# Attention with random features and a top-1 expert layer: the expert's choice starts ahead of a key maximum, and the second weight matrix of the first expert is rounded later, by ScalarE

## Chip, core and metric

One core of one Trainium2 chip runs the whole program. The metric is the device time of one execution in microseconds (us), the median of several runs. Engines are TensorE (PE), VectorE (DVE), ScalarE (ACT), GpSimd (POOL), and SyncE (SP), which only issues DMAs here.

## What is computed

The reference first computes attention with positive random features, for 8 batches, 8 heads, 576 tokens, head size 64 and 128 features. Its output, read as 4608 tokens of 512 numbers, goes through a layer of 8 experts of which each token uses one.

```python
def phi(x):
    proj = np.einsum('bhsd,md->bhsm', x, omega)
    h = proj - np.sum(x * x, axis=-1, keepdims=True) / 2.0
    h = h - np.max(h, axis=-1, keepdims=True)
    return np.exp(h) / np.sqrt(m)
...
kv = np.einsum('bhsm,bhsd->bhmd', k_p, v)
num = np.einsum('bhsm,bhmd->bhsd', q_p, kv)      # divided by den
...
logits = xn @ en.T / tau
expert_idx = np.argmax(logits, axis=1)
...
h = np.maximum(x[mask] @ w1[e], 0.0)
out[mask] = gate_w[mask, None] * (h @ w2[e])
```

## The kernel before

**Phase 1, attention.** A loop of 43 steps (`i` = 0 to 42) works on 36 tiles of 128 tokens. Step `i` projects key tile `i` and query tile `i - 6` (`proj`), takes the maxima of the features on VectorE (`maxima`, which writes `nmk` or `nmq`), and the exponentials on ScalarE (`feats`, which writes `ftk` or `ftq`). TensorE then transposes the query features (`qtr`, into the PSUM tile `nub`), ScalarE and VectorE copy one half each to SBUF (`qcopy`, which writes `qp`), and TensorE multiplies them with the key-value sums (`num`, into `nub` too). `num_out` divides on VectorE and writes the tokens of tile `i - 7` to a tile `xr` and their logits to `lg`. `kvmm` adds up the key-value sums. Every 4 or 5 steps one of these sums is closed: ScalarE copies it (`kvs`), GpSimd copies it again (`xgp<-kvs`), and TensorE transposes that (`kvtr`) ahead of the next `num`.

**The expert's choice.** Once three tiles have their logits (a group `g`, at steps 9, 12, 15, ...), `routed(g)` runs in pieces that are spread over the next steps. GpSimd adds the logits up (`raw`). VectorE takes their maximum and subtracts it (`mx`, then `raw<-raw,mx`: the first two operations), and GpSimd copies the result into the three `xr` tiles. VectorE picks the expert (three operations with `sel`), TensorE counts with `sel`, and VectorE adds the counts (`base`, `run`). GpSimd turns them into row numbers (four small operations on `base` and `pos`, then `posi`) and scatters each `xr` tile to the buffer `xs` in HBM, with one indirect DMA for each tile, in three successive steps. There are six `xr` buffers, so tile 24, for instance, is written where tile 18 was, once the scatter of tile 18 has landed:

```python
st["xr", i] = xr = p1.tile([P, PAY], F32, name=f"xr{i}", tag="xr", bufs=6)
```

**The first expert's weights.** After group 5 the expert with most tokens so far is known. From step 28 on, its eight pieces of weights of 128x1024 are loaded (`first_weights(n)`; even `n` are the first matrix, odd `n` the second). In the step behind the load, `first_split(n)` rounds each piece to a high part (`w1h` or `w2h`) and lets GpSimd subtract it from the piece in four operations of 128x256 to get the low part (`w1l`, `w2l`). `first_steps` multiplies the first two blocks of tokens with them: its matmuls fill up TensorE from step 37 on and go on behind the loop.

**The order.** Each engine works through its instructions in the order in which the program was written. Pieces that belong to a later step are put in lists: `mid` is played behind `qcopy`, `after` behind `num`, `then` behind the second maximum, ahead of the last key maximum, and `ends` at the end of the step. Pieces of one list run in the order in which they were put there.

**Phase 2, the experts.** From about 218 us on TensorE multiplies tokens with weights, step after step, until shortly before the end.

Of the kernel before, what the change touches and what calls it, by code (L numbers as in the profile page):

```python
# [16 lines left out]
AF = mybir.ActivationFunctionType  # L17
# [12 lines left out]
NTILE = NSB * TPS  # L30
G = 3
REG = N + P
GPICK = 5
# [4 lines left out]
NQ = 4  # L38
# [3 lines left out]
FILLS = 1, 2, 2, 2, 2, 0  # L42
FILL1, FILL2, FILL3 = 6, 11, 6
NSTAT = 38
WARM = 26
NSTEP = 64
XPE = 9
# [8 lines left out]
def attention_moe(ctx: ExitStack, tc: tile.TileContext, qT, kT, v1, omT, emb, tau, w1q, w2q, xs, out):  # L56
    nc = tc.nc
# [221 lines left out]
    with ExitStack() as c1:  # L279
# [243 lines left out]
        def first_weights(n):  # L523

            if n == 0:
                st["fe"] = nc.values_load(firsti[0:1, NPRE + 1 :], engines=[ET.SP], min_val=0, max_val=E - 1, skip_runtime_bounds_check_because=WHY)
            q, wn = n // 2, ("w1", "w2")[n % 2]
            st["rf", n] = raw = rawp.tile([P, F], F32, name=f"rf{n}", tag=f"raw_{wn}")
            nc.sync.dma_start(raw, W[wn][0].rearrange("(e q) p f -> e q p f", q=NQ)[ds(st["fe"], 1), q].rearrange("o p f -> (o p) f"))

        def first_split(n):
            q, (_, h, l) = n // 2, W[("w1", "w2")[n % 2]]
            raw = st["rf", n]
            if n % 2 == 0:
                nc.scalar.activation(h[:, 0, q, :], raw, AF.Copy)
            else:
                nc.vector.tensor_copy(h[:, 0, q, :], raw)
            for c in range(0, F, 256):
                c = slice(c, c + 256)
                nc.gpsimd.tensor_tensor(l[:, 0, q, c], raw[:, c], h[:, 0, q, c].bitcast(F32), op=ALU.subtract)  # L540

        def first_steps():


            new = lambda n, tag: ps.tile([P, 512], F32, name=f"fs_{n}", tag=tag, bufs=2 if tag == "px" else 1)
            hs = {}

            def up(t, a, cs, pa):
                for c in cs:
                    computed("w1", t, products(pa, pre_x[t], "w1", 0, [c], a, c == 0, c == 3))  # L550
                    yield
                if c == 3:
                    nc.scalar.activation(hs[t][:, a * 512 : (a + 1) * 512], pa, AF.Relu)

            def turn(t, a, tag):
                turned(hs[t], a * 512, new(f"h{t}{a}", tag), *(z[:, a * 512 : (a + 1) * 512] for z in pre_h[t]))
                yield

            def down(t, cs, po):
                for c in cs:  # L560
                    computed("w2", t, products(po, pre_h[t], "w2", 0, [c], 0, c == 0, c == 7))
                    yield
                if c == 7:
                    scaled(po, xgp[t], total[:, t : t + 1])
                    store(t, xgp[t])

            n2, total = few("n2", "p", NPRE), few("total", "p", NPRE)
            for t in range(NPRE):
                hs[t] = rawp.tile([P, F], F32, name=f"hp{t}", tag="raw_w1")
                turned(xgp[t], 0, new(f"x{t}", f"kv{t}"), *pre_x[t])  # L570
                squares(xgp[t], n2[:, t : t + 1], hs[t][:, 0:DM])
                yield
            nrm = root(gp, n2, NPRE, "p", nc.gpsimd)
            yield from up(0, 0, range(4), new("a00", "kv0"))
            norms(nrm)
            yield from up(0, 1, range(4), new("a01", "kv1"))
            for t in range(NPRE):
                exps(xgp[t], nrm[:, t : t + 1], total[:, t : t + 1])
            pa = new("a10", "kv0")
            yield from up(1, 0, range(2), pa)  # L580
            yield from turn(0, 0, "kv1")
            yield from up(1, 0, range(2, 4), pa)
            yield from turn(0, 1, "kv1")
            inverted(total)
            yield from up(1, 1, range(4), new("a11", "px"))
            po = new("o0", "kv0")
            yield from down(0, range(4), po)
            yield from turn(1, 0, "kv1")
            yield from turn(1, 1, "px")
            yield from down(0, range(4, 8), po)  # L590
            yield from down(1, range(8), new("o1", "kv1"))
# [47 lines left out]
        mid, after, then, ends = {}, {}, {}, {}  # L639
        at = lambda d, *key: d.setdefault(key, [])  # L640
        for i, f in ((1, emb0), (2, emb1), (4, emb2), (5, emb3)):
            at(ends, i).append((f,))
        later, fill = None, first_steps()

        def go(d, *key):
            for f, *a in d.pop(key, ()):
# [5 lines left out]
        for i in range(END + 1):  # L652
            iq = i - LAG
            st["now"] = i
            n = iq - 3 * GPICK - 7
            if 0 <= n < 2 * NQ:
                first_weights(n)
            if i < 2 or i >= 4:
                load(i + (4 if i < 2 else 2))
            if i in (3, 4):  # L660
                loadq(i - 3)
            loadq(iq + 2 if i > LAG - 1 else -1)
            if iq - 3 * GPICK - 6 == 6:
                prow = [nc.values_load(
                    firsti[0:1, t : t + 1], engines=[ET.SP], min_val=t * P, max_val=(E - 1) * REG + t * P,
                    skip_runtime_bounds_check_because=WHY) for t in range(NPRE + 1)]
                for t in range(NPRE):
                    xload(t, prow[t], xgp[t])
            ks, qs, ts, ss = i < NTILE, 0 <= iq < NTILE, 1 <= iq <= NTILE, 1 <= i <= NTILE
            one, two = [], []  # L670
            if ks and qs:
                one, two = [("k", i, 1, "px"), ("q", iq, 0, "px")], [("k", i, 0, "py"), ("q", iq, 1, "py")]
            elif ks:
                one = [("k", i, a, ("px", "py")[i % 2]) for a in range(2)]
            elif qs:
                two = [("q", iq, a, ("px", "py")[i % 2]) for a in range(2)]
            proj(*one)
            if ts:
                qtr(iq - 1)
            for p in one[:1]:  # L680
                maxima(*p)
            proj(*two)
            if ts:
                qcopy(iq - 1, 1, True)
                qcopy(iq - 1, 0, False)
            go(mid, i)
            for p in one[:1]:
                feats(*p)
            if i == END:
                next(fill)  # L690
            for p in one[1:] or two[:1]:
                maxima(*p)
            if ts:
                num(iq - 1)
            go(after, i)
            for p in two[1:]:
                maxima(*p)
            u = (i - 1) % TPS
            sums = [(j, a, b) for j, b in ([(i - 2, 1)] if u == 5 else []) + [(i - 1, int(u > 4))] for a in range(2)] if ss else []
            if i == LAG:  # L700
                for j, a, b in [x for x in sums if x[1]]:
                    kvmm(j, a, b)
                sums = [x for x in sums if not x[1]]
            go(then, i)
            for p in one[1:] if two else ():
                feats(*p)
            if one:
                for p in two[:1]:
                    maxima(*p)
            for x in sums:  # L710
                kvmm(*x)
            closed = ss and u in (4, 8)
            if closed and not qs:
                kv_closed((i - 1) // TPS, u // 4 - 1)
            if ts:
                num_out(iq - 1)
            for p in (two[::-1] if one else two) or one[1:]:
                feats(*p)
            if closed:
                sb, b = (i - 1) // TPS, u // 4 - 1  # L720
                if qs:
                    kv_closed(sb, b)
                at(mid, i + 1).append((kv_turn, sb, b))
                at(then if i >= LAG else after, i + 1).append((kv_turned, sb, b))
                at(then, i + 1).append((kv_logits, sb, b))
                at(ends, i + 1).append((kv_logits_out, sb, b))
            if ts and iq % G == 0 and iq < NTILE:
                steps = routed(iq // G - 1)
                next(steps)
                for d, key in ((ends, i + 1), (mid, i + 2) if i >= NTILE else (ends, i + 1), (after, i + 2), (ends, i + 2), (ends, i + 2), (ends, i + 3), (ends, i + 4)):  # L730
                    at(d, min(key, END)).append((next, steps, None))
            go(ends, i)
            if NTILE < i <= END:
                for _ in range(FILLS[i - NTILE - 1]):
                    next(fill)
            if 0 <= n < 2 * NQ:
                at(ends, i + 1).append((first_split, n))
        loop.close()
        assert not any((mid, after, then, ends)), (mid, after, then, ends)
        steps = routed(NTILE // G - 1)  # L740
# [179 lines left out]
    with tc.manual_schedule(engines={ET.PE, ET.Activation, ET.DVE, ET.Pool, ET.SP}):  # L920
        xt[NPRE] = pre_x[0]
        turn, ends = {}, NSTAT - 1
# [261 lines left out]
```

## Time and profile before

| | us |
|---|---|
| median of 3 runs (lowest, highest) | 662.74 (662.1, 663.9) |
| profiled execution, its own time | 658.2 |
| its span, first to last instruction | 656.4 |
| PE busy in the span | 631.7 (96%) |
| DVE busy | 497.3 (76%) |
| ACT busy | 416.9 (64%) |
| POOL busy | 328.5 (50%) |

The profiled execution is one run of its own. It was 4.5 us shorter than the median of the timed runs, and 1.8 us of its time lie outside of the span. The granted clock of TensorE was 0.996 of full speed over the span. The busy shares are means over two phases with different limits, so what one place of phase 1 is worth must be read there.

### The profile page before, as it was taken

To read this page: it belongs to the slowest core of one execution; us is meant where nothing else is said; L and a number is where in the kernel's file an instruction comes from. 1 tells how busy PE (TensorE), PEld (TensorE's weight loads), DVE (VectorE), ACT (ScalarE), POOL (GpSimd) and SP (SyncE) were. 2 spreads that over 40 slices of the span, in tenths; PEclk is the share of its full clock that TensorE was granted. 3 is DMA by queue.
4 is the path that set the end of the run, shared out by engine and by line. 5 is a ranking of instruction groups with operands and counts; after the bars stand their busy time and mean duration, and the time that the engine had idled before them with its cause. 6 is when DMAs were issued, how large, how long until landed. Compare 5 with 4: busy or idle time off the path is not lost. (4 is left out here: it accounts for less than half of the span.)

```text
span 656.4 us, 18641 instructions
## 1 busy us (share of the span) xinstructions
PE 631.7 (96%) x6339; PEld 532.1 (81%) x6340; DVE 497.3 (76%) x952; ACT 416.9 (64%) x1074; POOL 328.5 (50%) x414
## 2 busy tenths in 40 slices
PE   8999999998889999999999999999999999999993
PEld 7899999988877787888788888888888888888872
DVE  4789888899888736778787777777768787777771
ACT  6899899899877236645656565656555656565430
POOL 2013443448885425474556364646455554646352
PEclk9999999999999999999999999999999999999998
DMA  7547667678832388588898888978697878887710
GB/s 252 177 148 228 196 202 212 214 243 285 261 125 97 118 308 259 156 237 198 237 211 223 208 227 190 240 193 232 178 244 184 236 192 196 225 208 212 187 64 34
DMA packets 142362, 131.89 MB, mean 201 GB/s; under 512 B 106742, under 2 KB 106870, under 8 KB 142272
## 3 DMA queue, kind: packets, MB, share of 16 engines
q1 hardware_dynamic: 135808, 110.04, 62.8%
q0 software_dynamic: 6320, 20.38, 7.9%
q8 instruction: 57, 0.93, 0.6%
q10 hardware_dynamic: 144, 0.26, 0.2%
q14 instruction: 33, 0.27, 0.1%
HBM read 83.78 MB, written 21.97 MB: 161 GB/s over the span
## 5 line engine op out<-in xcount | busy, mean ns | idle before, releaser
L241 PE MATMUL nu<-w2h,hl 128*128 (+1 forms) x288 | 113.9, 395 | 0.4 <-DVE hl L948 0.4
L241 PE MATMUL nu<-w2h,hh 128*128 (+1 forms) x288 | 113.9, 396 | 0.0
L241 PE MATMUL nu<-w2l,hh 128*128 (+1 forms) x288 | 113.8, 395 | 0.0
L241 PE MATMUL pa<-w1h,xl 128*128 (+1 forms) x280 | 110.8, 396 | 0.4 <-DVE xl L947 0.4
L241 PE MATMUL pa<-w1h,xh 128*128 (+1 forms) x280 | 111.1, 397 | 0.0
L241 PE MATMUL pa<-w1l,xh 128*128 (+1 forms) x280 | 110.6, 395 | 0.0
L909 ACT ACTIVATE pl<-pa 128x512 uint16<-128x512 uint16 x68 | 40.1, 594 | 94.2 <-PE pa L241 56.0
L905 DVE TENSOR_REDUCE wd<-t 128x1024 uint16<-128x1024 uint16 x68 | 90.0, 1325 | 1.7 <-DMA t<-pl 1.7
L338 ACT ACTIVATE ftk<-pjk,nmk 128x128 f32<-128x128 f32 x288 | 84.9, 427 | 6.3 <-DVE nmk L331 6.0
L207 POOL TENSOR_TENSOR w1l<-raww,w1h 128x1024 f32 x34 | 83.7, 2461 | 7.4 <-DVE w1h L206 5.5
L905 DVE TENSOR_REDUCE pl<-pa 128x512 uint16<-128x512 uint16 x68 | 46.6, 688 | 51.6 <-ACT pl L909 51.5
L338 ACT ACTIVATE ftq<-pjq,nmq 128x128 f32<-128x128 f32 x288 | 80.0, 430 | 8.7 <-DVE nmq L331 7.8
L207 POOL TENSOR_TENSOR w2l<-raww,w2h 128x1024 f32 x34 | 82.1, 2415 | 2.4 <-issue 2.4
L327 PE MATMUL pjq<-om,qt 64*128 64x128 f32 x576 | 75.6, 283 | 1.1 <-ACT ftk L338 0.7
L327 PE MATMUL pjk<-om,kt 64*128 64x128 f32 x576 | 76.3, 285 | 0.3 <-DVE om L602 0.3
L944 ACT ACTIVATE hh<-wd 128x1024 fp32r<-128x1024 f32 x34 | 36.1, 1062 | 60.2 <-DVE wd L905 54.3
L327 PEld LDWEIGHTS pjk<-om,kt 64*128 64x128 f32 x576 | 65.1, 190 | 2.9 <-DVE om L602 0.6
L271 POOL DMA_INDIRECT y<-xgp x20 | 22.7, 1136 | 87.6 <-DVE xgp L248 84.1
L241 PEld LDWEIGHTS nu<-w2h,hl 128*128 128x128 f32 x288 | 54.0, 188 | 13.9 <-DVE hl L948 0.8
L327 PEld LDWEIGHTS pjq<-om,qt 64*128 64x128 f32 x576 | 63.9, 188 | 1.6 <-ACT ftk L338 0.9
L241 PEld LDWEIGHTS nu<-w2l,hh 128*128 128x128 f32 x288 | 54.1, 188 | 13.1
L241 PEld LDWEIGHTS nu<-w2h,hh 128*128 128x128 f32 x288 | 54.1, 188 | 13.0
(311 smaller groups left out, 1270.0 us busy)
## 6 DMA issues: line engine op xcount, KB each, us to landing
raww<-w1q SPq DMA_DIRECT2D x38, 512.0 KB, 3.9
raww<-w2q SPq DMA_DIRECT2D x38, 512.0 KB, 5.2
qt<-qT SPq DMA_DIRECT2D x36, 256.0 KB, 4.3
kt<-kT SPq DMA_DIRECT2D x35, 256.0 KB, 3.0
xgp<-xs SPq DMA_DIRECT2D x20, 260.5 KB, 2.8
xg<-xs SPq DMA_DIRECT2D x18, 260.5 KB, 2.9
rf<-w1q SPq DMA_DIRECT2D x4, 512.0 KB, 5.6
rf<-w2q SPq DMA_DIRECT2D x4, 512.0 KB
```

The costliest lines, as they stand in the source:

```text
L207: il = nc.gpsimd.tensor_tensor(at(l, dp), raw, at(h, dp).bitcast(F32), op=ALU.subtract)
L241: done.append(nc.tensor.matmul(dst, x[:, c * P : (c + 1) * P], ws.rearrange("p o f -> p (o f)"), start=(begin and i == 0 and k == 0), stop ...
L271: w = nc.gpsimd.indirect_dma_start(out=out, out_offset=bass.IndirectOffsetOnAxis(ap=xg[:, PAY - 1 : PAY].bitcast(I32), axis=0), in_=xg[:, ...
L327: nc.tensor.matmul(st["pj" + w, i, a][:, c, :], st[w, i][r, c, :], om[r, :], start=True, stop=True)
L338: nc.scalar.activation(ft[:, h, :], pj[:, h, :], AF.Exp, bias=nm[:, h : h + 1])
L905: nc.vector.tensor_reduce(to, src.unsqueeze(2), axis=AX.X, op=ALU.max)
L909: nc.scalar.activation(planes[1][:, o : o + 512], halved(src)[:, :, 1], AF.Copy)
L944: nc.scalar.activation(hh, wd[:, 0:F], AF.Relu)
```

## The change

The expert's choice: for groups whose choice starts before step 36, the first two operations on VectorE and the three copies on GpSimd move from the end of the step to the list `then`, ahead of the last key maximum. The weights: two tables now say in which step each piece is loaded (behind that step's keys, values and queries instead of ahead of them) and in which step and list it is split. The pieces of the first matrix keep their steps, the pieces of the second matrix are split in steps 37, 38, 40 and 41. ScalarE rounds all of them. As the splits are now entered into the lists before the loop starts, they run ahead of the other pieces of the same list.

```diff
+WLOAD = {28: (0,), 30: (2, 1), 32: (4, 3), 34: (6,), 39: (5,), 40: (7,)}
+WSPLIT = {0: (1, 29), 2: (1, 31), 4: (1, 33), 6: (1, 35), 1: (0, 37), 3: (0, 38), 5: (0, 40), 7: (0, 41)}
...
         def first_split(n):
             q, (_, h, l) = n // 2, W[("w1", "w2")[n % 2]]
             raw = st["rf", n]
-            if n % 2 == 0:
-                nc.scalar.activation(h[:, 0, q, :], raw, AF.Copy)
-            else:
-                nc.vector.tensor_copy(h[:, 0, q, :], raw)
+            nc.scalar.activation(h[:, 0, q, :], raw, AF.Copy)
...
-        later, fill = None, first_steps()
+        for n, (late, i) in WSPLIT.items():
+            at(ends if late else mid, i).append((first_split, n))
+        fill = first_steps()
...
-            n = iq - 3 * GPICK - 7
-            if 0 <= n < 2 * NQ:
-                first_weights(n)
             if i < 2 or i >= 4:
                 load(i + (4 if i < 2 else 2))
             if i in (3, 4):
                 loadq(i - 3)
             loadq(iq + 2 if i > LAG - 1 else -1)
+            for n in WLOAD.get(i, ()):
+                first_weights(n)
...
-                for d, key in ((ends, i + 1), (mid, i + 2) if i >= NTILE else (ends, i + 1), (after, i + 2), (ends, i + 2), (ends, i + 2), (ends, i + 3), (ends, i + 4)):
+                for d, key in ((then if i < NTILE else ends, i + 1), (mid, i + 2) if i >= NTILE else (ends, i + 1), (after, i + 2), (ends, i + 2), (ends, i + 2), (ends, i + 3), (ends, i + 4)):
                     at(d, min(key, END)).append((next, steps, None))
...
-            if 0 <= n < 2 * NQ:
-                at(ends, i + 1).append((first_split, n))
```

Three places show how instructions move. The first is GpSimd in steps 29 to 31. A number behind a name is that of the tile or group: `rf0` is piece 0 of the weights, `xr18` the tokens of tile 18, `base6` belongs to group 6. Before:

```order
L484 TENSOR_TENSOR base6_3628<-base6_3628,sel0_127 128x24
L449 TENSOR_TENSOR base6_3628<-base6_3628 128x3x4
L449 TENSOR_TENSOR base6_3628<-base6_3628 128x3x2
L449 TENSOR_TENSOR pos6_3632<-base6_3628 128x3
L494 CAST posi06_3636<-pos6_3632 128x1
L496 DMA xs<-xr18_3047,posi06_3636 38016x576
L540 TENSOR_TENSOR w1l_107<-rf0_3356,w1h_106 128x256 x4
L425 COPY xr23_3744<-ids_89 128x1
L449 TENSOR_TENSOR lg7_3472<-lg7_3472 128x3x32
```

The same place of the changed kernel:

```order
L539 TENSOR_TENSOR w1l_107<-rf0_3362,w1h_106 128x256 x4
L486 TENSOR_TENSOR base6_3631<-base6_3631,sel0_127 128x24
L451 TENSOR_TENSOR base6_3631<-base6_3631 128x3x4
L451 TENSOR_TENSOR base6_3631<-base6_3631 128x3x2
L451 TENSOR_TENSOR pos6_3635<-base6_3631 128x3
L496 CAST posi06_3639<-pos6_3635 128x1
L498 DMA xs<-xr18_3053,posi06_3639 38016x576
L427 COPY xr23_3744<-ids_89 128x1
L451 TENSOR_TENSOR lg7_3478<-lg7_3478 128x3x32
```

The four subtractions of piece 0 moved from behind the scatter of tile 18 to a place ahead of the whole chain that leads to it.

The second place is VectorE in step 31, from the key maximum to the query copy of step 32. Before:

```order
L331 TENSOR_REDUCE nmk_0_3855<-pjk_0_3811 128x4
L429 TENSOR_SCALAR rr_3876<-nub 128x8
L430 RECIPROCAL rr_3876<-rr_3876 128x8
L432 TENSOR_TENSOR xr_3873<-nub,rr_3876 128x2x4x64
L435 TENSOR_TENSOR lg_3875<-nub,rr_3876 128x64
L459 TENSOR_REDUCE mx_3896<-raw_3761 128x3
L460 TENSOR_TENSOR raw_3761<-raw_3761,mx_3896 128x24
L465 SCALAR_TENSOR_TENSOR sel_128<-raw_3761,iotm 128x24
L466 TENSOR_REDUCE mx_3896<-sel_128 128x3
L467 TENSOR_TENSOR sel_128<-iotm,mx_3896 128x24
L331 TENSOR_REDUCE nmk_1_3944<-pjk_1_3918 128x4
L405 COPY qp_0_3958<-nub 128x512
```

The same place of the changed kernel (`xr_3872` is tile 24 here, as `xr_3873` is before):

```order
L461 TENSOR_REDUCE mx_3843<-raw_3761 128x3
L462 TENSOR_TENSOR raw_3761<-raw_3761,mx_3843 128x24
L333 TENSOR_REDUCE nmk_0_3854<-pjk_0_3804 128x4
L431 TENSOR_SCALAR rr_3875<-nub 128x8
L432 RECIPROCAL rr_3875<-rr_3875 128x8
L434 TENSOR_TENSOR xr_3872<-nub,rr_3875 128x2x4x64
L437 TENSOR_TENSOR lg_3874<-nub,rr_3875 128x64
L467 SCALAR_TENSOR_TENSOR sel_128<-raw_3761,iotm 128x24
L468 TENSOR_REDUCE mx_3843<-sel_128 128x3
L469 TENSOR_TENSOR sel_128<-iotm,mx_3843 128x24
L333 TENSOR_REDUCE nmk_1_3939<-pjk_1_3913 128x4
L407 COPY qp_0_3953<-nub 128x512
```

The two operations on `mx` and `raw` went ahead of the key maximum; the casts `w2h<-rf`, which stood at the end of steps 30, 32, 34 and 36, are gone from this engine.

The third place is GpSimd in steps 35 and 36, up to the copy of the last key-value sum. Before:

```order
L484 TENSOR_TENSOR base8_4478<-base8_4478,sel0_127 128x24
L449 TENSOR_TENSOR base8_4478<-base8_4478 128x3x4
L449 TENSOR_TENSOR base8_4478<-base8_4478 128x3x2
L449 TENSOR_TENSOR pos8_4482<-base8_4478 128x3
L494 CAST posi08_4486<-pos8_4482 128x1
L496 DMA xs<-xr24_3873,posi08_4486 38016x576
L540 TENSOR_TENSOR w1l_107<-rf6_4228,w1h_106 128x256 x4
L425 COPY xr29_4564<-ids_89 128x1
L363 COPY xgp2_105<-kvs3_1_4581 128x2x4x64
```

The same place of the changed kernel:

```order
L539 TENSOR_TENSOR w1l_107<-rf6_4218,w1h_106 128x256 x4
L486 TENSOR_TENSOR base8_4464<-base8_4464,sel0_127 128x24
L451 TENSOR_TENSOR base8_4464<-base8_4464 128x3x4
L451 TENSOR_TENSOR base8_4464<-base8_4464 128x3x2
L451 TENSOR_TENSOR pos8_4468<-base8_4464 128x3
L496 CAST posi08_4472<-pos8_4468 128x1
L498 DMA xs<-xr24_3872,posi08_4472 38016x576
L427 COPY xr29_4545<-ids_89 128x1
L365 COPY xgp2_105<-kvs3_1_4562 128x2x4x64
```

Here too the subtractions, of piece 6, went ahead of the chain and its scatter; the copy of the key-value sum stays behind all of them.

## Rows read from the trace of the kernel before

**Rows 1.** Phase 2: its length, then PE, PEld, DVE, ACT, POOL busy, clock, DMA.

```profile
218.00:640.00 422.00, 420.59 (x1838) 337.65 (x1837) 314.38 (x490) 230.86 (x427) 220.98 (x120) 1.00 0.79 208
```

**Rows 2.** Waits of PE, 140 to 225 us: in total, times, longest.

```profile
PE nub L417 <- DVE qp L405: 4.0, 5, 1.7
```

**Rows 3.** Groups of instructions, 140 to 225 us: busy, mean ns, idle before.

```profile
L537 DVE CAST w2h<-rf 128x1024 fp32r<-128x1024 f32 x4 | 3.5, 862 | 0.0
```

**Rows 4.** Waits of ACT, 151 to 173 us (steps 30 to 33).

```profile
ACT qp L405 <- PE nub L400: 1.5, 2, 0.9
```

**Rows 5.** Timeline of POOL, steps 29 to 31: start, duration, idle before.

```profile
146.97 0.19 POOL L425 COPY xr<-ids 128x1 int32<-128x1 int32 x1 [3.38 <-DMA xs<-xr,posi]
148.04 0.23 POOL L484 TENSOR_TENSOR base<-base,sel 128x24 f32<-128x24 f32 x1 [0.89 <-DVE base L481]
...
150.23 1.05 POOL L496 DMA_INDIRECT xs<-xr,posi  x1 [0.86 <-POOL posi L494]
...
155.53 0.24 POOL L449 TENSOR_TENSOR raw<-lg 128x24 f32<-128x24 f32 x1
...
157.31 2.79 POOL L540 TENSOR_TENSOR w2l<-rf,w2h 128x256 fp32r<-128x256 f32 x4
```

**Rows 6.** Timeline of ACT, steps 29, 35: `w1h` is the rounding.

```profile
148.62 1.14 ACT L535 ACTIVATE w1h<-rf 128x1024 fp32r<-128x1024 f32 x1
...
179.78 1.14 ACT L338 ACTIVATE ftk<-pjk,nmk 128x128 f32<-128x128 f32 x4 [1.30 <-DVE nmk L331]
...
184.06 1.14 ACT L535 ACTIVATE w1h<-rf 128x1024 fp32r<-128x1024 f32 x1
```

**Rows 7.** Scatters `xs<-xr,posi` issued from 140 to 166 us, issue to landing.

```profile
DMA to landing us min/median/max: 5.5/5.8/6.5
```

**Rows 8.** The same of the scatters issued from 204 to 222 us.

```profile
DMA to landing us min/median/max: 2.7/2.8/2.8
```

**Rows 9.** Timeline of DVE, step 31.

```profile
157.82 0.69 DVE L432 TENSOR_TENSOR xr<-nub,rr 128x512 f32<-128x512 f32 x1
...
158.56 0.17 DVE L459 TENSOR_REDUCE mx<-raw 128x3 f32<-128x24 f32 x1
...
159.50 0.65 DVE L465 SCALAR_TENSOR_TENSOR sel<-raw,iotm 128x24 bf16<-128x24 f32 x1
...
160.39 0.18 DVE L467 TENSOR_TENSOR sel<-iotm,mx 128x24 bf16<-128x24 f32 x1
...
161.09 0.68 DVE L405 COPY qp<-nub 128x512 f32<-128x512 f32 x1
```

**Rows 10.** Timeline of DVE, end of step 34.

```profile
176.61 0.17 DVE L459 TENSOR_REDUCE mx<-raw 128x3 f32<-128x24 f32 x1
...
177.47 0.65 DVE L465 SCALAR_TENSOR_TENSOR sel<-raw,iotm 128x24 bf16<-128x24 f32 x1
...
178.46 0.69 DVE L537 CAST w2h<-rf 128x1024 fp32r<-128x1024 f32 x1
```

**Rows 11.** Timeline of POOL, steps 36 and 37.

```profile
185.37 1.05 POOL L496 DMA_INDIRECT xs<-xr,posi  x1 [0.56 <-POOL posi L494]
...
189.84 0.60 POOL L363 COPY xgp<-kvs 128x512 f32<-128x512 f32 x1
```

**Rows 12.** Timeline of PE, step 37.

```profile
190.49 0.66 PE L372 MATMUL kvtr<-ident,xgp 128*128 128x128 f32 x4 [0.32 <-POOL xgp L363]
```

**Rows 13.** Waits of ACT, 189 to 213 us (steps 37 to 41).

```profile
ACT ftq L338 <- DVE nmq L331: 6.1, 5, 1.8
```

**Rows 14.** Waits of POOL, 190 to 226 us.

```profile
POOL base L484 <- DVE base L481: 4.1, 2, 3.2
POOL xs L496 <- DVE runi L761: 3.2, 1, 3.2
```

**Rows 15.** Timeline of POOL behind the loop.

```profile
231.57 0.60 POOL L765 DMA_DIRECT2D xs<-w1l  x1 [5.08 <-DMA xgp<-xs]
```

**Rows 16.** Timeline of PE at the start of phase 2.

```profile
232.02 0.60 PE L227 MATMUL fs_x<-ident,xgp 128*128 128x128 f32 x4
```

## Prediction

> **What bounds the kernel now.** I read the chain that ended last first; it covers only the last microseconds, so the bound must be read by stage. The table of busy time by stretch shows phase 2: TensorE is busy for 420.59 of 422 us [rows 1]. Whatever phase 1 gains or loses is therefore carried to the end nearly whole, and the change touches phase 1 alone.
>
> In phase 1 I read the waits of each engine and then the timelines. Two views have to be held against each other. TensorE waits for VectorE's query copy (`qp`), 4.0 us in five waits [rows 2], and VectorE spends 3.5 us on the four casts that the change takes away [rows 3]. That looks like a gain. But from 151 to 173 us ScalarE has only two waits, 1.5 us together, both for TensorE [rows 4]: it goes through its exponentials and roundings without a pause, so most of what VectorE saves there meets ScalarE. The third engine to watch is GpSimd. It is far from busy on the whole, but in steps 28 to 37 it holds things that others need: the copy for `kvtr`, the sums `raw`, and the scatters that free the `xr` buffers. A copy into an `xr` tile has already stood still for 3.38 us, waiting for a scatter to land [rows 5].
>
> **The change, part by part.** The sum is made against the profiled execution (658.2 us) and put on the median of the runs shown, 662.74 us, which lies 4.5 us above it.
>
> *Casts taken from VectorE.* In steps 30, 32 and 36 I count them at nothing, since ScalarE or TensorE ends the waits there [rows 4]. If that cover were gone, each would be worth its 0.86 us [rows 3]. In step 34 the cast is on the path: ScalarE then waits 1.30 us for the key maximum behind it [rows 6]. Before that maximum stand `mx` and `raw<-raw,mx` (176.61 to 177.47), a `sel` of 0.65 us and the cast of 0.69 us [rows 10]. The first pair moves ahead at a cost of about 0.4 us, `sel` no longer meets a split on GpSimd (undisturbed, an operation of that size took 0.18 us [rows 9]) and the cast is gone: some 1.5 us less, of which ScalarE can use the 1.30 us that it waits. **-1.3 us.**
>
> *First two operations ahead of the key maximum, steps 10 to 28.* VectorE does the same work; the maximum and what follows come about 0.4 us later, and `sel` follows at the old time. Up to step 28 I find no wait that this lengthens by more than 0.1 us a group. Seven groups: between 0 and +0.7 us, taken as 0, since the query copy of the next step does not move.
>
> *Split of piece 0 ahead of the scatter of tile 18 (step 29).* This is the largest term. GpSimd was at the chain `base` at 148.04 us and issued the scatter at 150.23 [rows 5]. Now the split comes first, and it must wait for ScalarE's rounding, which ends at 148.62 + 1.14 = 149.76 [rows 6]. Four subtractions take 2.79 us when nothing disturbs them [rows 5]: 152.6. The chain up to the issue took 150.23 - 148.04 = 2.19 us: 154.8. Around here a scatter lands 5.5 to 6.5 us after its issue, 5.8 in the middle [rows 7]: 160.6. VectorE writes tile 24 into the same buffer two steps later, at 157.82 before [rows 9]. It will stand there until 160.6, and GpSimd too, whose copy into tile 24 waits for the same landing. Behind the write, the distance to the query copy of step 32 was 161.09 - 157.82 = 3.27 us; `mx` and `raw` (158.56 to 159.50, 0.94 us) are gone from it, but `sel` stays slow, because the split of piece 2, held up by the same landing, then runs beside it [rows 9]. So the copy comes at 160.6 + 2.33 = 162.9 instead of 161.09. **+1.8 us.** Upper end: a landing after 6.5 us (+0.7) and a second `sel` operation slowed from 0.18 to 0.65 us (+0.5). Lower end: the shortest landing that any row shows, 2.8 us [rows 8], at 157.6: no wait at all, 0. I take the middle of the landings in this stretch, since the second matrix is loaded in the same stretch as before and now right behind the first, so it is no emptier.
>
> The Trainium skill, page "DMA: Bandwidth & Descriptors", section "Anatomy of one DMA — SWDGE (gpsimd) path", gives such a DMA a fixed 2.0 us plus its bytes over 436e3 per us; for 128 rows of 521 numbers that is an estimate of 2.6 us. The quiet stretch agrees (2.8), the stretch in question does not (5.8). By the page the scatter would land at 157.4 and the sum would be that of the second rival below.
>
> *Split of piece 6 ahead of the chain (step 35).* Rounded at 184.06 + 1.14 = 185.20 [rows 6], split until 188.0, the chain 1.9 us more (2.19 less 0.30 for the shorter pause of 0.56 ahead of the issue), the issue 1.05, one small copy 0.2: the copy for `kvtr` starts at 191.1 instead of 189.84 [rows 11]. TensorE already waits 0.32 us for it [rows 12], and the next `num` stands behind `kvtr`. **+1.3 us.** The split that went away from step 34 does not help, as GpSimd caught up before.
>
> *Four roundings more on ScalarE, steps 37 to 41.* At 1.14 us each [rows 6] they stand between `qp` and `ftq`, where ScalarE waits 6.1 us in five waits for the query maximum [rows 13]. About 1.2 us a step cover about 1.1: **0**, and up to 0.5 us where the cover is short.
>
> *Four splits in steps 37 to 41 on GpSimd.* One takes the place of the split that stood in step 37, three are added: 3 x 2.79 = 8.4 us. GpSimd's idle time there is 4.1 + 3.2 = 7.3 us [rows 14]. So the last scatters come about 1.1 us later, and with them the load of the third block of tokens, which waits for them all. That block landed at about 231.5 (GpSimd's DMA at 231.57 waited for it [rows 15]), and TensorE takes it up at 232.02 [rows 16]: 0.5 us of slack. **+0.5 us.** Operations on VectorE that meet these splits: between 0 and twice 0.47 us; **+0.3 us.**
>
> Sum: -1.3 + 1.8 + 1.3 + 0.5 + 0.3 = **+2.6 us**, 665.3 us.
>
> **Rivals.** *The scatter lands in time.* At anything under about 4 us the buffer is free when VectorE comes. Then `mx` still waits for `raw`, whose end (155.77 before [rows 5]) moves by the 4.6 us of the scatter less the 2.79 us or more of the split that stood between, to about 157.3; this takes away what the shorter `sel` gives, and the query copy is about where it was. The sum is -1.3 + 1.3 + 0.5 + 0.3 = +0.8 us, 663.5 us. For it speaks [rows 8], against it [rows 7].
>
> *VectorE is the bound of steps 30 to 36 after all (faster).* Then its four casts come back whole: -3.5 us [rows 3], 659.2 us. For it speak TensorE's waits [rows 2], against it ScalarE without pauses [rows 4]. It is decided at step 35: the gain must still stand when `kvtr` starts, so the copy on GpSimd must not come after 189.84 less the gain.
>
> *ScalarE waits for the late loads.* The last two pieces are loaded in steps 39 and 40, one step ahead of their rounding. If they take as long as loads did in the crowded stretch (5.8 us as the scatters [rows 7]) instead of a step, ScalarE stands for about 1.5 us ahead of `ftq`; with the second case that is +2.3 us, 665.0 us. Against it: DMA is quiet there [rows 8].
>
> **How the numbers follow.** About 0.3%, 2.0 us, is what a measurement of this kernel can tell from no change. Chances: forecast 0.55, scatter in time 0.27, VectorE the bound 0.11, late loads 0.07. The forecast's own range is 664.0 to 667.0: the landing and the slow `sel` at their upper ends (+1.2) and the tail whole (+0.5) above, a landing at 5.5 us and no disturbance by splits (-0.6), with part of the chain's pause hidden, below. About a fifth of it lies under +2.0. Slower: 0.8 x 0.55 + 0.6 x 0.07 = 0.48. Faster: the third case, and it alone: 0.10. The rest, 0.42, is no change to be told. The range for 8 in 10 takes in the second case with its own spread down to 661.6 and ends above at 667.0; it leaves out the third case and a few mishaps above.
>
> **What would show it.** In the profile after: VectorE's write to `xr` in step 31 with an idle stretch of about 2 us ended by a scatter's DMA; GpSimd's first split right behind ScalarE's first rounding; no wait of 1.3 us for the key maximum in step 35; `kvtr` waiting for GpSimd for 1 us or more in step 37; ScalarE's waits for the query maximum in steps 37 to 41 nearly gone. The prediction is wrong if the scatter of tile 18 lands within about 4 us, or if its write in step 31 has no such wait.

## The result and the profile after

The change makes the kernel slower: 666.84 us (median; 665.38 to 669.33) against 662.84 us (662.1 to 663.9) of the kernel before on the same chip, a ratio of 1.0059, 95% interval 1.0037 to 1.0081. The prediction named 665.3 us, with a range of 661.6 to 667.0, and slower as the likeliest outcome. But the 4.0 us are not the sum that it worked out. They are a loss of some 9 us in the weights part and a gain of some 5 us in the part that it had counted at nothing.

A number that comes up throughout: the runs fell on several chips, and the kernel before takes 663 us on some of them (662.8, 663.6 and 663.1 in the three comparisons) and 657 us on others (657.05 and 656.8). Below they are called a 663 chip and a 657 chip, and medians are compared on one chip alone. Each chip on record served one comparison, so whether the chip itself makes the difference, or something else of that comparison, is not shown; the names only sort the runs. The profiled execution shown ahead of the prediction (658.2 us) looks like one of a 657 chip; the experiments show why this matters.

The profile after was taken on an execution of 669.33 us (span 667.5), 2.5 us above its median. Line numbers are 2 higher than before. First VectorE in step 31, its timeline (start, duration, idle before and what ended it), the answer to [rows 9]:

```profile
159.11 0.18 DVE L461 TENSOR_REDUCE mx<-raw 128x3 f32<-128x24 f32 x1 [0.28 <-POOL raw L451]
159.32 0.18 DVE L462 TENSOR_TENSOR raw<-raw,mx 128x24 f32<-128x24 f32 x1
159.43 0.68 DVE L333 TENSOR_REDUCE nmk<-pjk 128x4 f32<-128x512 f32 x1
...
166.01 0.69 DVE L434 TENSOR_TENSOR xr<-nub,rr 128x512 f32<-128x512 f32 x1 [5.59 <-DMA xs<-xr,posi]
...
167.17 0.39 DVE L469 TENSOR_TENSOR sel<-iotm,mx 128x24 bf16<-128x24 f32 x1
...
168.08 0.67 DVE L407 COPY qp<-nub 128x512 f32<-128x512 f32 x1
```

The two moved operations stand ahead of the last key maximum (159.11). The write to `xr`, which did not wait before, now waits 5.59 us for a scatter. GpSimd's timeline of steps 29 to 31 shows which, beside [rows 5]:

```profile
152.18 2.79 POOL L539 TENSOR_TENSOR w1l<-rf,w1h 128x256 fp32r<-128x256 f32 x4 [3.40 <-ACT w1h L536]
...
156.82 1.05 POOL L498 DMA_INDIRECT xs<-xr,posi  x1 [0.57 <-POOL posi L496]
...
165.97 0.19 POOL L427 COPY xr<-ids 128x1 int32<-128x1 int32 x1 [4.92 <-DMA xs<-xr,posi]
```

The split of piece 0 comes first, the scatter of tile 18 behind it at 156.82. The copy into tile 24, which needs that scatter to have landed, goes on at 165.97, 9.15 us after the issue. TensorE stands still meanwhile; its waits from 143 to 228 us (total, times, longest) answer to [rows 2] and [rows 12]:

```profile
PE nub L402 <- DVE lg L437: 6.4, 2, 5.8
...
PE kvtr L374 <- POOL xgp L365: 1.1, 1, 1.1
PE nub L419 <- DVE qp L407: 0.8, 2, 0.6
```

The wait for the query copy fell from 4.0 to 0.8 us, and others took its place: 5.8 us of step 31 in one piece, and 1.1 us for `kvtr` in step 37 (0.32 before). In steps 37 to 41 ScalarE, the answer to [rows 13]:

```profile
ACT ftq L340 <- DVE nmq L333: 1.8, 3, 1.2
...
ACT w2h L536 <- DMA rf<-w2q: 0.5, 1, 0.5
```

Phase 2 lasts as long as before: from the query copy of step 42 (225.93) to the end of the span (667.5) it is 441.6 us, against 442.1. All that differs lies in phase 1.

### The profile page after: what moved, and what is told of

It is laid out like the page before. It is cut to its first block, busy times and chain, and to the rows that moved or that the text cites. A ratio compares the mean times of both kernels' runs of the same rounds, so it can differ in the third digit from the quotient of the medians.

```text
span 667.5 us, 18640 instructions
## 1 busy us (share of the span) xinstructions
PE 634.8 (95%) x6339; PEld 534.0 (80%) x6340; DVE 492.3 (74%) x948; ACT 420.2 (63%) x1078; POOL 325.3 (49%) x414
```

## The experiments

All code lines are against the kernel that the heading names. Experiments 1 to 4 ran on one 663 chip (before: 663.62 us, 662.63 to 666.33).

**1. Changed kernel, the four splits of the first matrix behind the routed pieces again.**

```diff
+BEHIND = 0, 2, 4, 6
-            at(ends if late else mid, i).append((first_split, n))
+            if n not in BEHIND:
+                at(ends if late else mid, i).append((first_split, n))
...
+            for n in BEHIND:
+                if WSPLIT[n][1] == i:
+                    at(ends, i).append((first_split, n))
             go(ends, i)
```

> The changed kernel, with the four splits of the first matrix put behind the routed pieces of their steps again, as they stood before. Theory: the 4.0 us come from the order on GpSimd (the split of piece 0 ahead of the scatter of tile 18, that of piece 6 ahead of the copy for kvtr); then both waits go, step 31 takes about 6 us and not 11.5, and the median falls by 4 to 6 us, to 661 to 663. Rival, the first two operations ahead of the key maximum cost about 2 us by step 28: 664 to 665. Rival, the roundings and splits in steps 37 to 41 cost the time: 665 or more.

Measured: 660.12 us, ratio to before 0.9948 (0.993 to 0.9966), a little under the time expected. The order alone is worth more than the whole loss; the changed kernel with the old order beats the kernel before. The profile has neither wait: step 31 takes 5.50 us, and `kvtr` does not wait. It was taken on the slowest of the eight executions, though (662.79 us), and has another loss: steps 32 and 33 take 17.70 us, against 12.05 in experiment 2. TensorE stands still for 2.06 us in step 32, for a load of queries, and its clock falls (last section).

**2. Kernel before, with the two operations moved and nothing else.**

```diff
-                for d, key in ((ends, i + 1), (mid, i + 2) if i >= NTILE else (ends, i + 1), (after, i + 2), (ends, i + 2), (ends, i + 2), (ends, i + 3), (ends, i + 4)):
+                for d, key in ((then if i < NTILE else ends, i + 1), (mid, i + 2) if i >= NTILE else (ends, i + 1), (after, i + 2), (ends, i + 2), (ends, i + 2), (ends, i + 3), (ends, i + 4)):
```

> The kernel before with one part of the change alone: the first two operations of the expert's choice ahead of the last key maximum. Theory: nothing to tell, 662.5 to 663.5; the 2.1 us by which the changed kernel was behind at step 28 in its profiled execution are its spread. Rival, the move costs about 2 us in steps 10 to 28: 664.5 to 665.5.

Measured: 658.77 us, ratio 0.9923 (0.9903 to 0.9943). Both expectations fail, and in sign: the move gains 4.9 us.

**3. Changed kernel without that move.**

```diff
-                for d, key in ((then if i < NTILE else ends, i + 1), (mid, i + 2) if i >= NTILE else (ends, i + 1), (after, i + 2), (ends, i + 2), (ends, i + 2), (ends, i + 3), (ends, i + 4)):
+                for d, key in ((ends, i + 1), (mid, i + 2) if i >= NTILE else (ends, i + 1), (after, i + 2), (ends, i + 2), (ends, i + 2), (ends, i + 3), (ends, i + 4)):
```

> The changed kernel without the move of the first two operations: the weights part alone. Theory: it carries the whole loss, 666 to 668. Rival, the move costs 2 us: 664.5 to 665.5.

Measured: 672.72 us, ratio 1.0135 (1.0115 to 1.0154). The weights part alone loses 9.1 us, more than either expectation allowed. The two parts account for the change: 0.9923 x 1.0135 = 1.0057, against 1.0059 measured.

**4. Changed kernel, the split of piece 0 alone behind the routed pieces:** experiment 1 with a shorter list.

```diff
-BEHIND = 0, 2, 4, 6
+BEHIND = 0,
```

> The changed kernel, with the split of piece 0 alone put behind the routed pieces of step 29. Theory: the wait of 5.6 us in step 31 goes; what the profiled step 31 lost (11.5 against 6.2 us) and step 32 (1.2 us) comes back in part, 662 to 664; the wait for the copy for kvtr in step 37 (1.1 us) stays. Rival, the stall of step 31 would have been made up elsewhere (GpSimd's load sets the end of phase 1): 665.5 or more.

Measured: 661.07 us, ratio 0.9958 (0.9942 to 0.9975). By the two ratios, both of 663 chips, this one place gives back 1.0059 - 0.9958 = 0.0101, 6.7 us. Its profile has no wait in step 31 and the old wait in step 37; VectorE's timeline, then TensorE's waits from 185 to 220 us:

```profile
157.88 0.69 DVE L435 TENSOR_TENSOR xr<-nub,rr 128x512 f32<-128x512 f32 x1
...
159.74 0.68 DVE L408 COPY qp<-nub 128x512 f32<-128x512 f32 x1
```

```profile
PE kvtr L375 <- POOL xgp L366: 1.6, 1, 1.6
```

Between 4 and 1 stand the splits of pieces 2, 4 and 6: 0.0010, 0.7 us, less than the two intervals can tell apart.

Why does a move of two small operations gain 4.9 us where the profile before showed no wait that it could shorten? The program of experiment 3 is, up to step 27, that of the kernel before, and it was profiled on the 663 chip. VectorE's waits there, from 27 to 137 us:

```profile
DVE rr L431 <- PE kva L355: 2.3, 2, 1.2
DVE rr L431 <- ACT ftq L340: 2.0, 3, 1.1
...
DVE rr L431 <- PE nub L419: 1.0, 2, 0.5
DVE rr L431 <- PE nub L386: 1.0, 1, 1.0
```

Together 6.3 us ahead of `rr`, the first operation on a finished `num`. Step 13 of the same profile shows what stands behind that wait, and below it step 13 of experiment 2:

```profile
60.67 0.17 DVE L431 TENSOR_SCALAR rr<-nub 128x8 f32<-128x8 f32 x1 [0.52 <-PE nub L419]
...
61.90 0.17 DVE L461 TENSOR_REDUCE mx<-raw 128x3 f32<-128x24 f32 x1
62.11 0.18 DVE L462 TENSOR_TENSOR raw<-raw,mx 128x24 f32<-128x24 f32 x1
...
63.50 0.67 DVE L407 COPY qp<-nub 128x512 f32<-128x512 f32 x1
```

```profile
59.04 0.17 DVE L459 TENSOR_REDUCE mx<-raw 128x3 f32<-128x24 f32 x1
59.24 0.18 DVE L460 TENSOR_TENSOR raw<-raw,mx 128x24 f32<-128x24 f32 x1
...
59.94 0.15 DVE L429 TENSOR_SCALAR rr<-nub 128x8 f32<-128x8 f32 x1
...
62.47 0.68 DVE L405 COPY qp<-nub 128x512 f32<-128x512 f32 x1
```

In the old place the pair stands between the wait and the query copy of the next step, with no pause behind it. In the new place it fills the time in which VectorE would wait. The same waits in experiment 2:

```profile
DVE rr L429 <- PE kva L353: 2.3, 2, 1.1
...
DVE rr L429 <- PE nub L384: 0.7, 1, 0.7
```

3.0 us instead of 6.3; the repetition, experiment 12, has 3.0 us as well.

**5 and 6. Kernel before, unchanged, profiled again.** These, 7 and 8 ran on a 657 chip (before: 657.05 us, 655.43 to 658.24).

> The kernel before, unchanged, profiled once more: its first profiled execution (658.2) lay under all of its timed runs. Theory: in an execution of its usual time, 663, the steps in which the expert's choice stands ahead of the query copy (13, 16, 19, 22, 25, 28) are longer than in the first profile by 0.5 to 1 us each, as the weights part alone shows them (13: 5.82 against 5.17; 16: 5.81 against 5.15; 22: 6.42 against 5.23; 25: 5.86 against 5.15). Rival: the 5 us lie in phase 2 or ahead of step 7, and the steps are as in the first profile.

> The kernel before, unchanged, a third profiled execution, for the spread between executions. The same expectations as for the second.

Measured: 658.01 and 658.18 us, so not executions of 663 us as hoped; but they show the same thing from the other side. VectorE's waits ahead of `rr`, 27 to 138 us, in experiment 5:

```profile
DVE rr L429 <- ACT ftq L338: 0.9, 3, 0.3
DVE rr L429 <- PE nub L384: 0.2, 1, 0.2
```

1.1 us against 6.3 for the same program. From the query copy of step 7 to that of step 28 it takes 138.27 - 27.32 = 110.95 us here, 111.20 in experiment 6 and 111.08 in the profile ahead of the prediction, but 142.48 - 27.25 = 115.23 in experiment 3. These are the rows:

```profile
27.32 0.68 DVE L405 COPY qp<-nub 128x512 f32<-128x512 f32 x1
138.27 0.68 DVE L405 COPY qp<-nub 128x512 f32<-128x512 f32 x1
```

```profile
27.25 0.68 DVE L407 COPY qp<-nub 128x512 f32<-128x512 f32 x1
142.48 0.68 DVE L407 COPY qp<-nub 128x512 f32<-128x512 f32 x1
```

The steps named in the expectation (13, 16, 19, 22, 25) are longer by 0.6 to 1.2 us each between experiments 5 and 3. With the move the stretch takes 138.33 - 27.08 = 111.25 us on the 663 chip: 4.0 of the 4.9 us lie in these steps. No profile of the kernel before itself was taken on a 663 chip; experiment 3 stands in for it up to step 27.

**7. Changed kernel, the load of piece 1 one step later.**

```diff
-WLOAD = {28: (0,), 30: (2, 1), 32: (4, 3), 34: (6,), 39: (5,), 40: (7,)}
+WLOAD = {28: (0,), 30: (2,), 31: (1,), 32: (4, 3), 34: (6,), 39: (5,), 40: (7,)}
```

> The changed kernel with the load of piece 1 one step later (31 and not 30), so that it no longer stands right behind that of piece 2. Theory: the scatter of tile 18 landed 9.1 us after its issue since both loads ran beside it; apart from that load it lands after 5.5 to 6.5 us, the wait in step 31 falls from 5.6 to about 3 us, and the median to 663.5 to 665. Rival: the landing is late for another reason (the scatters, key and value loads alone): 666 to 667.5, with a wait of 5 us or more in step 31.

Measured: 661.57 us, ratio 1.0057 (1.0038 to 1.0077). The expected times were for a 663 chip and can't be held against a 657 chip; the wait in step 31 can: 3.00 us, as the theory has it. Experiments 9 and 10 put both kernels on one chip.

**8. Kernel before, the two operations moved in steps 10 to 25 alone:** experiment 2 with another bound.

```diff
-                for d, key in ((then if i < NTILE else ends, i + 1), (mid, i + 2) if i >= NTILE else (ends, i + 1), (after, i + 2), (ends, i + 2), (ends, i + 2), (ends, i + 3), (ends, i + 4)):
+                for d, key in ((then if i < 27 else ends, i + 1), (mid, i + 2) if i >= NTILE else (ends, i + 1), (after, i + 2), (ends, i + 2), (ends, i + 2), (ends, i + 3), (ends, i + 4)):
```

> The kernel before with the two operations ahead of the last key maximum in steps 10 to 25 alone; in steps 28, 31 and 34 they stay where they were. Theory: the gain of the move (4.9 us) is made in the steps before the weights, some 0.7 us in each of six: 659 to 660.5. Rival: it is made in steps 28 to 34, where VectorE casts and meets GpSimd's splits: 662.5 or more.

Measured: 655.93 us, ratio 0.9984 (0.9974 to 0.9995). On a 657 chip the move gains 1.1 us in these steps: there is little wait to fill. The times named were those of a 663 chip, so this run does not test the rival; the 4.0 us by place, under 5 and 6, speak against it.

**9 and 10. The changed kernel beside the one with the later load**, on another 657 chip (before: 656.8 us, 655.19 to 658.24). The edit is that of experiment 7.

> The changed kernel, unchanged, beside the kernel with the later load. The kernel before took 663.6 us on one chip and 657.05 on another; on a chip of the second kind the sum of the parts (split order about +6, late splits +1.4, the move about -1.5) gives a ratio of 1.008 to 1.010, on one of the first kind 1.006 as measured. Rival: the chip changes the level alone, and the ratio is 1.006 on both.

> The changed kernel with the load of piece 1 one step later, on the same chip as the changed kernel. Theory: the two loads side by side lengthen the landing of the scatter of tile 18; with the later load the wait in step 31 is 3 us and not 5.6, and the time 2 to 3.5 us under that of the changed kernel. Rival: the load makes no difference to be told (within 1 us); the landing is late because of the scatters, the key and value loads.

Measured: 664.11 us, ratio 1.0089 (1.0057 to 1.0121), and 660.5 us, ratio 1.005 (1.0033 to 1.0067). The ratio of 9 is where the sum of the parts had it, but its interval takes in the rival's 1.006. One of its six executions took 658.23 us, at a granted clock of 0.995 where the other five have 0.989 to 0.992, so the loss is not in every execution; that one has no profile. The later load takes 3.6 us off the median. The two intervals overlap a little, so this rests on the traces as well. First experiment 9: SyncE issues both loads as GpSimd issues the scatter of tile 18, and VectorE waits 6.21 us (timelines of SP's queue, POOL, DVE).

```profile
152.54 0.34 SPq L531 DMA_DIRECT2D rf<-w1q  x1
153.14 0.34 SPq L531 DMA_DIRECT2D rf<-w2q  x1
```

```profile
153.14 1.05 POOL L498 DMA_INDIRECT xs<-xr,posi  x1 [0.56 <-POOL posi L496]
...
162.93 0.19 POOL L427 COPY xr<-ids 128x1 int32<-128x1 int32 x1 [5.55 <-DMA xs<-xr,posi]
```

```profile
162.98 0.69 DVE L434 TENSOR_TENSOR xr<-nub,rr 128x512 f32<-128x512 f32 x1 [6.21 <-DMA xs<-xr,posi]
```

Then experiment 10, the same rows:

```profile
151.88 0.34 SPq L531 DMA_DIRECT2D rf<-w1q  x1
...
156.95 1.26 SPq L531 DMA_DIRECT2D rf<-w2q  x1
```

```profile
152.64 1.05 POOL L498 DMA_INDIRECT xs<-xr,posi  x1 [0.56 <-POOL posi L496]
...
159.41 0.19 POOL L427 COPY xr<-ids 128x1 int32<-128x1 int32 x1 [2.54 <-DMA xs<-xr,posi]
```

```profile
159.45 0.69 DVE L434 TENSOR_TENSOR xr<-nub,rr 128x512 f32<-128x512 f32 x1 [3.20 <-DMA xs<-xr,posi]
```

From issue to landing it is 162.93 - 153.14 = 9.8 us with both loads beside it, and 159.41 - 152.64 = 6.8 us with the second load 4.3 us behind the scatter. The scatter itself is the same. The other profiles agree: 9.15 us in the profile after and 9.55 in experiment 3, with both loads; 6.6 us in experiment 7.

**11 and 12. The changed kernel with order and loads mended, beside the move alone**, on a 663 chip (before: 663.11 us, 661.1 to 665.02). 12 is experiment 2 again; 11 is experiment 1 with two loads moved.

```diff
-WLOAD = {28: (0,), 30: (2, 1), 32: (4, 3), 34: (6,), 39: (5,), 40: (7,)}
+WLOAD = {28: (0,), 30: (2,), 31: (1,), 32: (4,), 33: (3,), 34: (6,), 39: (5,), 40: (7,)}
```

> The changed kernel with both mends: the four splits of the first matrix behind the routed pieces of their steps, and the loads of pieces 1 and 3 one step later. Theory: what is left against the move alone is the late roundings and splits in steps 40 and 41, 1 to 2 us: ratio to the kernel before 0.994 to 0.996 on a chip where that takes 663, 0.998 to 1.001 on one where it takes 657. Rival: with order and loads mended the casts off VectorE pay too, and it is under the move alone by 1 us or more.

> The move of the two operations alone, once more beside the mended kernel. Theory: it beats the kernel before on every chip, by 4.9 us again where that takes 663, by 1 to 2 us where it takes 657. Rival: on a chip of 657 it makes no difference (within 0.5 us).

Measured: 659.74 us, ratio 0.9952 (0.9936 to 0.9968), and 657.37 us, ratio 0.9912 (0.9893 to 0.9932). With the order mended the later loads bring nothing more that the medians show (0.9948 in experiment 1). What is left of the weights part still costs 2.4 us against the move alone, so as a whole it does not pay. Where it costs them is shown in part only, since the profile of 11 is of its shortest execution (657.11 us): steps 28 to 36 take 49.28 us there against 50.63 in 12, and steps 37 to 41 take 27.20 against 26.11. Casts and late splits were not run apart. The fastest version on 663 chips is the kernel before with the move alone. The whole move ran on 663 chips only; on a 657 chip the part of it in experiment 8 is 1.1 us faster.

## Why the prediction came near, and what was wrong in it

The profiles put the time in its places. Lengths in us between query copies, and to the end of the span:

| steps | before, 657 chip (exp. 5) | changed, 657 chip (exp. 9) | move alone, 663 chip (exp. 2) | changed, 663 chip |
|---|---|---|---|---|
| 7 to 27 | 110.95 | 109.52 | 111.25 | 112.52 |
| 28 to 30 | 16.93 | 15.93 | 16.70 | 16.41 |
| 31 to 33 | 18.12 | 25.24 | 18.14 | 24.58 |
| 34 to 36 | 16.08 | 16.11 | 15.77 | 16.03 |
| 37 to 41 | 25.01 | 28.06 | 26.16 | 28.78 |
| 42 to end | 441.8 | 441.5 | 440.8 | 441.6 |

On the 657 chips the lengths add up to +7.5 between the first two columns, where the medians differ by 7.3 us. In the last column TensorE waits 1.10 us in step 22, as in no other profile here.

**First two operations ahead of the key maximum, "taken as 0": this step failed.** The range given for it reached from nothing to +0.7 us and had no gain in it. Measured for the whole move: -4.9 us, and -5.7 us in the repetition, on 663 chips; of this -4.0 us in steps 7 to 27, where a 657 chip has -1.4 us. The step reasoned from a profile of 658.2 us, in which VectorE hardly waits ahead of `rr`, about a kernel whose timed runs were at 662.1 to 663.9. The prediction noted that the median lay 4.5 us above the sum's base and put the sum on it unchanged. By experiment 3 nearly all of these 4.5 us are waits in the very steps that the move touches: the stretch from step 7 to 27 is 115.23 - 110.95 = 4.3 us longer on a 663 chip.

**Split of piece 0 ahead of the scatter, +1.8 us: the mechanism was right, the size was off.** Buffer, waiting operation and place are as predicted, and the issue came when the sum had it (5.36 us after the query copy of step 30, 156.82 - 151.46; predicted 154.8 - 149.11 = 5.69). The mis-sized term is the landing: 5.8 us, "no emptier" with the second load behind the first, where it took 9.15 and 9.8 us. Experiments 9 and 10 show that the second load, issued 0.6 us behind the first, makes 3.0 us of that. The rows from which 5.8 was taken had one load of 512 KB a step. The prediction saw that the second load would stand right behind the first and didn't let it raise the upper end beyond 6.5 us. By the rule of the Trainium skill that the prediction weighed (page "DMA: Bandwidth & Descriptors", section "Anatomy of one DMA — SWDGE (gpsimd) path", an estimate of 2.6 us) there would have been no wait; the trace is further from it than forecast. The same page of the Trainium skill, section "SWDGE vs HWDGE vs iDMA", says that a DMA engine takes its queues in turn, those of GpSimd's transfers and those of the others; a longer landing beside more load fits it, but no run here shows the turns.

**The query copies behind the stall.** Steps 31 and 32 together lost 12.18 + 6.26 - 6.09 - 5.23 = 7.1 us between experiments 5 and 9. 1.0 us of that is step 32, which the sum did not have: TensorE's clock, below. `sel` was hardly slowed (one of three operations, 0.39 for 0.18), although the splits of piece 2 did run beside all three, from 166.11 us on. At 0.69 us each (2.77 / 4) the first two subtractions ended at about 166.80 and 167.49: the first `sel` began at 166.75, and the third, the slow one, ended at 167.56.

**Casts off VectorE, -1.3 us.** The wait for the key maximum in step 35 is gone, as predicted. Step 34 went from 6.72 to 5.97 us, -0.75, with the move alone to 6.12. In experiment 11, with order and loads mended, it takes 5.19 us, and there the forecast gain is whole (against 6.49 us in experiment 5). What holds it back in the changed kernel is not shown.

**Split of piece 6, +1.3 us.** `kvtr` waits 1.1 us (0.32 before), 1.6 in experiment 4: +0.8 to +1.3. The medians of experiments 1 and 4 don't resolve it.

**Roundings, splits and tail in steps 37 to 41, 0 + 0.3 + 0.5 us.** Too small, and at the wrong place. The tail is not later (441.5 against 441.8). The loss is in steps 38 to 41: 21.62 against 19.30 us, +2.3, by experiments 9 and 5. Step 40 of the profile after shows how. VectorE waits for a scatter that was issued at 211.15, behind two splits, and landed 7.0 us later; in [rows 8] the scatters of this stretch took 2.7 to 2.8 us. SyncE had issued the loads of pieces 5 and 7 at 210.64, right ahead of it, as it did at tile 18. In experiment 9 the same scatter took 6.4 us. No run moved these two loads. And two small operations take 0.78 and 0.74 us beside a split (0.25 and 0.15 us before).

```profile
218.17 0.69 DVE L434 TENSOR_TENSOR xr<-nub,rr 128x512 f32<-128x512 f32 x1 [0.73 <-DMA xs<-xr,posi]
...
219.11 0.78 DVE L462 TENSOR_TENSOR raw<-raw,mx 128x24 f32<-128x24 f32 x1
219.81 0.74 DVE L257 TENSOR_SCALAR rt_p<-rt_p 128x2 f32<-128x2 f32 x1
```

```profile
206.39 2.79 POOL L539 TENSOR_TENSOR w2l<-rf,w2h 128x256 fp32r<-128x256 f32 x4
...
211.15 1.04 POOL L498 DMA_INDIRECT xs<-xr,posi  x1 [0.56 <-DVE nmq L333]
...
218.43 2.77 POOL L539 TENSOR_TENSOR w2l<-rf,w2h 128x256 fp32r<-128x256 f32 x4
```

The Trainium skill, page "SBUF — State Buffer", section "SBUF: two separate sides", says that of a VectorE operation with two inputs from SBUF and a GpSimd instruction that reads SBUF, the one that starts first holds the other back for the whole of its length. The 0.78 us of the subtraction `raw<-raw,mx`, against one of GpSimd's at 0.69 us, agrees. The other small operation has one tensor input, and the rule for two inputs does not cover it.

**What was to show it.** Each sign came: the split right behind the first rounding, the wait of `xr` in step 31 (5.59 us for about 2), `kvtr` waiting over 1 us, no wait for the key maximum in step 35. ScalarE's waits for the query maximum fell from 6.1 to 1.8 us, not to nothing. The signs showed the mechanisms of the weights part; none was named for the move.

**The rivals.** The scatter did not land in time. The casts were not what bound steps 30 to 36: of the 3.5 us, steps 28 to 36 show 1.3 at most, in experiment 11 against the move alone. ScalarE waits 0.5 us for a late load, not 1.5; but the stretch that [rows 8] showed quiet was so no longer, as these loads now ran in it. None of the rivals had the gain that came, since all kept the move at 0.

So the sum of +2.6 us came near +4.0 because two errors offset each other: 6.5 us too little loss in the weights part (2.6 for 9.1), and a gain of 4.9 us that was left out. On a 657 chip, the kind that the profile resembled, the change costs 7.3 us by the medians of experiment 9.

## What to carry to other kernels

When the profiled execution lies outside the range of the timed runs, the difference is time that its rows don't show, and a term that those rows put at 0 can be as large as that difference; look for the steps in which the waits could be. A transfer's duration taken from a stretch holds only for what is in flight there: a load that the change puts beside it belongs into its bound. Before a piece of work is put ahead of a scatter, ask which buffer the scatter frees and which engine stands at that buffer two steps later.

## What the runs showed of the hardware

On some chips the same program took 657 us and on others 663 (one comparison on each chip), and single instructions take the same time on both (the `xr` write 0.69 us, the query copy 0.68). The waits between engines differ. In experiment 3, on a 663 chip, TensorE has pauses of up to 0.4 us for which the profile shows no cause, in steps 13, 16, 22 and 25 (its waits from 27 to 137 us; experiment 5 has none):

```profile
PE kva L355 <- issue: 1.2, 4, 0.4
```

Experiment 2, on the same chip with the move, has none either, so the chip alone does not make them. Whether these pauses set off the waits ahead of `rr`, and what makes them, stays open.

TensorE's clock fell in the stall. TensorE had stood still for 5.77 us in step 31, up to 166.89; from 165.0 to 168.1 us the granted clock is 0.50, the level of 1.2 GHz. In step 32 behind it the granted clock is 0.78 in the mean, between the levels of 2.4 and 1.2 GHz; TensorE is busy throughout that step, which takes 6.23 us instead of 5.05. The columns are length, busy times of PE, PEld, DVE, ACT and POOL, clock, DMA share and GB/s:

```profile
168.10:174.30 6.20, 6.20 (x126) 5.91 (x126) 4.58 (x12) 5.39 (x20) 2.93 (x7) 0.78 0.44 105
```

The same matmuls of the projection take 347 ns in the mean in step 32 and 281 ns in step 34 (groups by form):

```profile
L329 PE MATMUL pjq<-om,qt 64*128 64x128 f32 x19 | 3.7, 347 | 0.0
```

```profile
L329 PE MATMUL pjq<-om,qt 64*128 64x128 f32 x18 | 2.6, 281 | 0.0
```

In experiment 4, without the wait, the clock from 161 to 170 us is 1.00. A stall of TensorE thus cost more than its own length here: 1.0 to 1.2 us in the step behind it, for 6.4 us in experiment 9 and 5.8 us in the profile after. A shorter stall was enough in the profile of experiment 1: TensorE stood still for 2.06 us, up to 165.41, and from there to 170 us the granted clock is 0.50. Steps 32 and 33 took 8.57 and 9.13 us, against 5.21 and 6.84 in experiment 2; in the second of them TensorE is busy throughout (columns as above):

```profile
160.00:168.30 8.30, 6.05 (x115) 5.65 (x113) 4.29 (x11) 5.20 (x20) 5.15 (x12) 0.80 0.86 300
168.30:177.50 9.20, 9.20 (x181) 8.42 (x179) 5.30 (x12) 5.89 (x19) 3.07 (x8) 0.81 0.45 153
```
